# Pinning router setup, conversion starts, two weight splits and the head's load-dependent steps in a scheduled kernel

## Chip, cores and metric

The kernel runs on one core of a Trainium2 chip. The metric is device time in microseconds of one execution; a run gives one such time, and versions are compared by the median of several runs. A core has five engines that each work through an instruction list of their own in order: PE (matmuls; PEld is its weight loads), DVE (vector), ACT (activations), POOL (a second vector engine) and SP, which here issues all DMA transfers. An instruction that waits for another engine or for a transfer holds up everything behind it on its own engine.

## What is computed

Three stages, on 4 x 576 = 2304 tokens of width 512. Attention: for each batch and head, band attention (each query sees the keys less than 4 positions away) plus attention on q, k and v averaged in fours, repeated to full length. Then a softplus MLP with float64 weights, then a top-1 mixture of 8 experts:

```python
x = attn_out.transpose(0, 2, 1, 3).reshape(2304, 512)      # local + downsampled attention
h = x @ w_in; g = np.maximum(h, 0) + np.log1p(np.exp(-np.abs(h))); x = g @ w_out
logits = x @ w_gate + modality_bias[modality_id]; e_idx = argmax(logits)
out[mask] = gate_w[mask] * (np.maximum(x[mask] @ w1[e], 0) @ w2[e])      # for each expert e
```

## The kernel before

**Stages.** Attention is cut into jobs: `Down` (averaged attention of two heads, 16 jobs) and `Local` (band attention of two heads over 192 queries, 48 jobs). Each job has six steps (`st_T`, `st_S`, `st_E`, `st_N`, `st_Ta`, `st_PV`) that are written in the program with fixed lags, so several jobs are in flight. The MLP works on 6 blocks of 384 tokens; a block has 16 chunks of 128 hidden units, each with `mlp_H` (first product and softplus inputs), `mlp_g` (softplus) and `mlp_Y` (second product). Attention of later tokens is woven between the chunks. The expert stage follows.

**The head.** Until `started[0]` is set, only attention of batch 0 and the first of batch 1 is written, with a few conversions near the end. Batch 0 is transposed by PE; from batch 1 on `trans` uses DVE's transpose (line 166), straight from the loaded `qr` and `kr` tiles. A Local job's scores go PE (line 311) -> DVE lines 317 and 319 (mask and maximum) -> ACT line 325 (exponentials) -> DVE 329 and 330 -> POOL 331 (normalise) -> PE 336 (transpose) -> DVE 339 -> PE 344 (product with v, tile `lv`) -> DVE 360.

**Conversion.** The MLP's weights arrive as float64. `from_f64` makes float32 of a 128 x 512 chunk from its integer halves, with one ACT step (line 439) and four DVE steps (lines 440 to 443). 32 chunks, alternating between `wi` and `wo`, must pass before the last chunk of block 0. The raw chunks share six buffers (tag `raw`) with the `qr`, `kr` and `vr` loads of batches 1 to 3, so a load can wait for the conversion, transpose or sum that last read its buffer. `lv` has three buffers, freed by line 344.

**Splits.** From block 1 on every operand is split in a high and a low part (`split`, lines 475 to 480: ACT copies the high part, POOL subtracts for the low part), and a product is three matmuls. Block 0 uses plain float32 matmuls for its first product (line 579) and for half of its second (line 619).

**What sets the order.** The program is written in one order, but the tile framework schedules it: an instruction may move ahead of others on its engine when a timing model in the framework says that its inputs are there. `tc.keep_in_program_order(ins)` forbids this for one instruction: it stays behind the one that was written before it on its engine. Buffers are handed out by the schedule too, so a moved instruction also changes which load waits for what.

Of the kernel before, what the change touches and what calls it, by code (L numbers as in the profile page):

```python
# [9 lines left out]
F32 = mybir.dt.float32  # L10
F32R = mybir.dt.float32r
I32 = mybir.dt.int32
U32 = mybir.dt.uint32
AF = mybir.ActivationFunctionType
ALU = mybir.AluOpType
AX = mybir.AxisListType
# [4 lines left out]
E, FE = 8, 1024  # L21
# [5 lines left out]
NB = NT // TB  # L27
NTT = NT // 128
# [23 lines left out]
NATIVE = 1  # L52
# [3 lines left out]
def band_attention__softplus_mlp__top1_moe(  # L56
# [14 lines left out]
    nc = tc.nc  # L71
    V, A, G, T = nc.vector, nc.scalar, nc.gpsimd, nc.tensor
# [17 lines left out]
    wg = const.tile([128, CC, 32], F32, name="wg")  # L90
    V.memset(wg, 0.0)
    bias_b = const.tile([128, 2, E], F32, name="bias_b")
    bterm = const.tile([128, NTT, E], F32, name="bterm")
# [8 lines left out]
    wi = wpool.tile([128, NC1, CC, 128], F32, name="wi")  # L102
# [3 lines left out]
    def ahead(n):  # L106

        return tc.high_priority(n) if n else nullcontext()
# [12 lines left out]
    class Down:  # L121
# [28 lines left out]
        def pre(self):  # L150
            self.vs = apool.tile([SDH, 2, 2, D], F32, tag="vs", name="vs", bufs=4)
            x = self.raw[2].rearrange("p h a r d -> p (h a) r d")
            o = self.vs.rearrange("p a h d -> p h a d")
            if 4 <= self.b * NPAIR + self.hp < 16:
                G.tensor_tensor(out=x[:, :, 0:2], in0=x[:, :, 0:2], in1=x[:, :, 2:4], op=ALU.add)
                for h in range(2):
                    hs = slice(2 * h, 2 * h + 2)
                    G.tensor_tensor(out=o[:, h], in0=x[:, hs, 0], in1=x[:, hs, 1], op=ALU.add)
            else:
                V.tensor_reduce(out=o, in_=self.raw[2].rearrange("p h a r d -> p h a d r"), axis=AX.X, op=ALU.add)  # L160

        def trans(self, i):

            t = apool.tile([128, S], F32, tag=("qT", "kT")[i], name="qkT", bufs=4)
            if self.b >= PE_TRANSPOSED:
                V.transpose(t, self.raw[i].rearrange("p n d -> p (n d)"))
                return t
            half = RT // 2
            for g in range(2):
                ps = pa("pT")  # L170
                for r in range(half):
                    T.transpose(ps[:, r * RP:(r + 1) * RP], self.raw[i][:, g * half + r].rearrange("p h d -> p (h d)"),
                                ident[:RP, :RP])
                warm(ps)
                o = t.rearrange("m (p r) -> m r p", r=RT)[:, g * half:(g + 1) * half, :]
                x = ps[:, :half * RP].rearrange("m (r p) -> m r p", r=half)
                (A.copy if i or g else V.tensor_copy)(o, x)
            return t
# [81 lines left out]
    def warm(ps):  # L260

        if 4 <= nloc[0] < 12:
            for i in range(1):
                T.matmul(ps[:, 384:384 + 128], ident, ident[:, :128], start=True, stop=True)

    def pa(name):

        if not started[0]:
            nps[0] += 1
            if nps[0] % 2:  # L270
                return psy.tile([128, 512], F32, tag="py", name=name)
        return psa.tile([128, 512], F32, tag="pa", name=name)

    started = [False]
# [158 lines left out]
    def from_f64(raw, dst, on_g):  # L433

        lo, hi = raw[:, :, 0], raw[:, :, 1]
        t = mlp.tile([128, 512], I32, tag="cva", name="cva", bufs=2)
        A.activation(t.bitcast(F32), hi.bitcast(F32), AF.Abs)
        (G if on_g else V).tensor_scalar(t.bitcast(F32), t.bitcast(F32), F64_LEAST, None, ALU.max)  # L440
        V.tensor_scalar(t, t, 3, 0x3FFFFFF8, ALU.logical_shift_left, ALU.bitwise_and)  # L441
        V.scalar_tensor_tensor(t, hi, -0x40000000, t, ALU.bitwise_and, ALU.bitwise_or)  # L442
        V.scalar_tensor_tensor(dst.bitcast(I32), lo, 29, t, ALU.logical_shift_right, ALU.bitwise_or)
# [21 lines left out]
    def conv_to(n):  # L465
        while cpos[0] < min(n, len(conv)):
            i = cpos[0]
            load_raw(i + 2)
            kind, c = conv[i]
            with ahead(0 if started[0] else -50):  # L470
                from_f64(raws.pop(i), wi[:, c].rearrange("p c f -> p (c f)") if kind == "i" else wo[:, c, :], i < 0)
            cpos[0] += 1
            load_raw(i + 2)

    def split(src, tag):
        w = mlp.tile([128, 2] + list(src.shape)[1:], F32R, tag=tag, name=tag, bufs=2)
        with ahead(0):
            A.copy(w[:, 0], src)  # L478
            G.tensor_tensor(out=w[:, 1], in0=src, in1=w[:, 0].bitcast(F32), op=ALU.subtract)  # L479
        return w  # L480

    wis, wos = {}, {}

    def split_wi(n, c):
        if n < NATIVE:
            return
        wis[n, c] = split(wi[:, c] if n < NB else mo["w1"][:, :, c * 128:(c + 1) * 128], "wis")

    def plain_g(n, c):

# [2 lines left out]
    def split_wo(n, c):  # L493
        if plain_g(n, c):
            return
        wos[n, c] = split((wo if n < NB else mo["w2"])[:, c, :], "wos")
# [2 lines left out]


    def router_setup():
        nc.sync.dma_start(out=wg[:, :, :E], in_=w_gate.rearrange("(c p) e -> p c e", p=128))
        nc.sync.dma_start(out=bias_b.rearrange("p m e -> p (m e)"),
                          in_=mod_bias.rearrange("(o m) e -> o (m e)", o=1).to_broadcast([128, 2 * E]))
        ids = mlp.tile([NTT, 128, 2], I32, tag="raw", name="ids", bufs=RAWB)
        idf = mlp.tile([NTT, 128], F32, tag="cvs", name="idf", bufs=2)
        nc.sync.dma_start(out=ids.rearrange("p t w -> p (t w)"), in_=modality.bitcast(I32).rearrange("(p t) -> p t", p=NTT))
        V.tensor_copy(idf, ids[:, :, 0])
        ps = psa.tile([128, 512], F32, tag="pa", name="pI")
        T.transpose(ps[:, :NTT], idf, ident[:NTT, :NTT])  # L510
        is_m = const.tile([128, 2, NTT, 1], F32, name="is_m")
        bt = mlp.tile([128, NTT, E], F32, tag="cvs", name="bt", bufs=2)
        for m in range(2):
            V.tensor_scalar(is_m[:, m, :, 0], ps[:, :NTT], float(m), None, ALU.is_equal)
            G.tensor_tensor(out=bt if m else bterm, in0=is_m[:, m].to_broadcast([128, NTT, E]),
                            in1=bias_b[:, m:m + 1, :].to_broadcast([128, NTT, E]), op=ALU.mult)
        G.tensor_tensor(out=bterm, in0=bterm, in1=bt, op=ALU.add)

    ybuf = {}
# [114 lines left out]
    mo = {}  # L634
# [63 lines left out]
    def quad_weights(q):  # L698

        w1t = mo["w1"]  # L700
        ops = wset[q] = wfree.pop(0)
        tmp = mlp.tile([128, 4, 2, 128], F32, tag="wis", name="wtmp", bufs=2)
        f0, f1 = slice(q * 128, (q + 1) * 128), slice(FE // 2 + q * 128, FE // 2 + (q + 1) * 128)
        a11, a12, a21, a22 = w1t[:, 0:2, f0], w1t[:, 2:4, f0], w1t[:, 0:2, f1], w1t[:, 2:4, f1]

        def split(o, n, src):
            hi = ops[:, 0, o:o + n].rearrange("p o c f -> p (o c) f")
            lo = ops[:, 1, o:o + n].rearrange("p o c f -> p (o c) f")
            A.copy(hi, src)
            G.tensor_tensor(out=lo, in0=src, in1=hi.bitcast(F32), op=ALU.subtract)  # L710

        split(P11, 2, w1t[:, :, f0])
        V.tensor_tensor(out=tmp[:, 0], in0=a21, in1=a22, op=ALU.add)
        V.tensor_tensor(out=tmp[:, 1], in0=tmp[:, 0], in1=a11, op=ALU.subtract)
        split(S1, 2, tmp[:, 0:2].rearrange("p o c f -> p (o c) f"))
        V.tensor_tensor(out=tmp[:, 2], in0=a11, in1=a21, op=ALU.subtract)
        V.tensor_tensor(out=tmp[:, 3], in0=a12, in1=tmp[:, 1], op=ALU.subtract)
        split(S3, 2, tmp[:, 2:4].rearrange("p o c f -> p (o c) f"))
        split(P22, 1, a22)
# [94 lines left out]
    for st in range(12 + LAG):  # L814
        attn_to(pre_end[st])
        if st >= C0 - 5 + LAG:
            conv_to((st - C0 + 5 - LAG) * CR // 4 + 1)
        if st == 9 + LAG:
            split_wi(0, 0)
# [16 lines left out]
    for i, (n, c) in enumerate(seq[:NMLP]):  # L836
# [19 lines left out]
        if i + 1 < NMLP:  # L856
            split_wi(*seq[i + 1])
        else:
            ws = wpool.tile([128, 2, 2, NOP, 2, 128], F32R, tag="wi", name="ws")
            wfree += [ws[:, o] for o in range(2)]  # L860
# [15 lines left out]
        if n == 1 and c == 0:  # L876
            router_setup()
# [93 lines left out]
    p, q, pos_q = stages[-1]  # L971
# [57 lines left out]
```

## Time and profile before

| | |
|---|---|
| median of 3 runs | 795.28 us (795.06 to 795.6) |
| the profiled execution | 798.25 us, of which the span of instructions 796.2 us |
| busy in the span | PE 752.5, DVE 551.7, POOL 472.6, ACT 451.8 us |
| PE idle by stretch | 59:65 us: 5.8; 126:158: 4.4; 212:500: 1.2 |

The span runs from the first to the last instruction; all positions are us from its start. The granted clock of PE is a share of its full speed: 0.50 is 1.2 GHz, 1.00 is 2.4 GHz.

### The profile page before, as it was taken

The page shows a single profiled execution, that of the slowest core. Times are in us where ns is not written, and L with a number is a line of the kernel's source. Part 1 is how long each engine was busy: PE and PEld are TensorE (multiplying, and loading weights), DVE is VectorE, ACT ScalarE, POOL GpSimd, SP SyncE. Part 2 cuts the span into 40 slices and gives each one's busy share as a digit, 9 for nine tenths or more (in the row PEclk, how much of TensorE's full clock was granted, in tenths as well). Part 3 has the DMA queues.
Part 4 walks back from the last instruction along what each step waited for, and adds up shares of the span by engine and source line. Part 5 has one row for each costly group of instructions (what it writes and reads, how often), then busy time and mean ns, then how long its engine had stood idle before and what let it go on. Part 6 is the DMA issues. An engine that isn't in the chain of part 4 may idle for free.

```text
span 796.2 us, 13871 instructions
## 1 busy us (share of the span) xinstructions
PE 752.5 (95%) x4917; PEld 658.4 (83%) x4918; DVE 551.7 (69%) x1103; ACT 451.8 (57%) x1164; POOL 472.6 (59%) x451
## 2 busy tenths in 40 slices
PE   5886998899999999999999999999989999999994
PEld 4664655579799989899999999999977889899893
DVE  6979999967885787988654675556996385275221
ACT  5835566656566646666565656475646265355332
POOL 3435623757776666867566666666689366455541
PEclk9866999999999999999999999999999999999998
DMA  8849666415100251301000100080102022002002
GB/s 195 189 92 274 186 209 178 83 23 116 26 12 16 64 88 31 68 22 51 2 12 12 52 2 1 1 331 1 40 1 79 21 61 80 0 1 80 1 0 84
DMA packets 111448, 55.46 MB, mean 70 GB/s; under 512 B 89594, under 2 KB 102412, under 8 KB 111372
## 3 DMA queue, kind: packets, MB, share of 16 engines
q1 hardware_dynamic: 111371, 54.50, 25.7%
q8 instruction: 41, 0.67, 0.4%
q14 instruction: 36, 0.29, 0.1%
HBM read 45.05 MB, written 9.44 MB: 68 GB/s over the span
## 4 chain that ended last, share of the span: by engine, by line
PE 69%; DVE 17%; issue 4%; ACT 3%; DMA 3%; POOL 2%; SPq 1%; DVEq 0%; POOLq 0%; ACTq 0%
PE py L622 18%; PE ph L582 18%; PE py L913 12%; PE ph L764 9%; PE pO L344 2%; PE pS L311 2%; DVE cva L442 2%; PE ph L579 2%; PE pA L336 2%; DVE cva L440 1%; DVE g L604 1%; PE pS L210 1%; DVE cva L441 1%; DVE g L605 1%; DMA vr<-in_v_dram 1%
## 5 line engine op out<-in xcount | busy, mean ns | idle before, releaser
L622 PE MATMUL py<-g,wos 128*128 128x384 f32 x1056 | 209.8, 341 | 7.2 <-ACT wos L478 4.0
L622 PEld LDWEIGHTS py<-g,wos 128*128 128x128 f32 x1056 | 181.9, 188 | 14.1 <-ACT wos L478 5.2
L582 PE MATMUL ph<-xT,wis 128*128 128x384 f32 x960 | 184.3, 339 | 0.4 <-POOL wis L479 0.4
L582 PEld LDWEIGHTS ph<-xT,wis 128*128 128x128 f32 x960 | 166.3, 188 | 2.7 <-POOL wis L479 1.0
L479 POOL TENSOR_TENSOR wos<-wo,wos 128x512 fp32r<-128x512 f32 x88 | 124.0, 1410 | 40.5 <-ACT wos L478 37.3
L479 POOL TENSOR_TENSOR wis<-wi,wis 128x512 fp32r<-128x512 f32 x80 | 107.1, 1340 | 53.0 <-ACT wis L478 46.4
L588 ACT ACTIVATE ga<-ph 128x384 f32<-128x384 f32 x96 | 46.7, 486 | 72.3 <-PE ph L582 62.6
L603 DVE SCALAR_TENSOR_TENSOR ga<-ph,ga 128x384 f32<-128x384 f32 x88 | 48.4, 550 | 47.5 <-ACT ga L590 47.2
L769 DVE TENSOR_TENSOR u<-ph,u 128x384 f32<-128x384 f32 x60 | 33.2, 555 | 60.3 <-PE ph L764 60.1
L764 PE MATMUL ph<-xs,ws 128*128 128x384 f32 x378 | 73.6, 337 | 1.3 <-DVE u L769 0.9
L325 ACT ACTIVATE ls<-ls,lst 128x70 f32<-128x70 f32 x144 | 49.3, 344 | 43.9 <-DVE lst L319 38.6
L478 ACT CAST wos<-wo 128x512 fp32r<-128x512 f32 x88 | 54.2, 617 | 33.7 <-PE py L622 32.3
L764 PEld LDWEIGHTS ph<-xs,ws 128*128 128x128 f32 x378 | 67.0, 188 | 5.1 <-DVE u L769 1.3
L605 DVE TENSOR_TENSOR g<-ga,g 128x384 fp32r<-128x384 f32 x80 | 69.5, 868 | 1.6
L913 PE MATMUL py<-wos,gs 128*128 128x512 f32 x270 | 68.2, 394 | 0.3 <-ACT gs L773 0.3
L331 POOL TENSOR_TENSOR ls<-ls,lst 128x210 f32<-128x210 f32 x48 | 31.4, 656 | 54.7 <-DVE lst L330 36.8
L604 DVE CAST g<-ga 128x384 fp32r<-128x384 f32 x80 | 58.4, 730 | 4.5 <-PE py L622 0.9
L913 PEld LDWEIGHTS py<-wos,gs 128*128 128x128 f32 x270 | 50.1, 188 | 10.0 <-issue 0.6
L590 ACT ACTIVATE ga<-ga 128x384 f32<-128x384 f32 x96 | 50.3, 524 | 2.0
L589 ACT ACTIVATE ga<-ga 128x384 f32<-128x384 f32 x96 | 50.4, 525 | 0.5
L479 POOL TENSOR_TENSOR wos<-w2s,wos 128x512 fp32r<-128x512 f32 x24 | 33.2, 1388 | 27.5 <-ACT wos L478 27.5
L478 ACT CAST wis<-wi 128x512 fp32r<-128x512 f32 x80 | 48.9, 611 | 0.4 <-PE ph L582 0.4
(163 smaller groups left out, 1293.4 us busy)
## 6 DMA issues: line engine op xcount, KB each, us to landing
raw<-in_moe_w_in_dram SPq DMA_DIRECT2D x16, 512.0 KB
raw<-in_moe_w_out_dram SPq DMA_DIRECT2D x16, 512.0 KB
lv<-in_v_dram SPq DMA_DIRECT2D x72, 70.0 KB
vr<-in_v_dram SPq DMA_DIRECT2D x16, 288.0 KB
ydram<-y SPq DMA_DIRECT2D x12, 384.0 KB
yb<-ydram SPq DMA_DIRECT2D x12, 384.0 KB
out_dram<-ob SPq DMA_DIRECT2D x18, 256.0 KB
qr<-in_q_dram SPq DMA_DIRECT2D x48, 72.0 KB
```

The source lines that it names most:

```text
L325: A.activation(s[:, i, :], s[:, i, :], AF.Exp, bias=st[:, 0, i], accum_out=st[:, 1, i])
L478: A.copy(w[:, 0], src)
L479: G.tensor_tensor(out=w[:, 1], in0=src, in1=w[:, 0].bitcast(F32), op=ALU.subtract)
L582: T.matmul(ps[:, :TB], wt[:, w, cc, :], xT[n][:, x, cc, :], start=(i == 0), stop=(i == 3 * CC - 1))
L589: A.activation(a, a, AF.Exp, scale=-1.0)
L590: A.activation(a, a, AF.Ln, bias=1.0)
L603: V.scalar_tensor_tensor(a, ps[:, :TB], 0.0, a, ALU.max, ALU.add)
L604: (A.copy if n < 1 else V.tensor_copy)(g[:, 0, :], a)
L605: (G if n < 1 else V).tensor_tensor(out=g[:, 1, :], in0=a, in1=g[:, 0, :].bitcast(F32), op=ALU.subtract)
L622: T.matmul(yps[n][dc][:, :TB], w[:, a, dsl], g[:, b, :], start=(c == 0 and i == 0), stop=(c == NC1 - 1 and i == 2))
L764: T.matmul(ps[:, :TB], ops[:, w, a, cc, :], xop[p, x][:, l, cc, :], start=i == 0, stop=i == 5)
L913: T.matmul(yps[n][t], g[:, a, t * 128:(t + 1) * 128], w[:, b, :], start=first and c == q and i == 0, stop=last and c == q + NQ and i == 2)
```

## The change

Pins are put on: the three loads of `router_setup` and its cast and multiplications; the first (ACT) step of every float64 conversion; the two splits of block 1's first two chunks; and, in the head, the first addition of the v sums, the v reductions on DVE and DVE's transposes. No arithmetic is changed.

```diff
@@ pre, trans
-                G.tensor_tensor(out=x[:, :, 0:2], in0=x[:, :, 0:2], in1=x[:, :, 2:4], op=ALU.add)
+                ins = G.tensor_tensor(out=x[:, :, 0:2], in0=x[:, :, 0:2], in1=x[:, :, 2:4], op=ALU.add)
+                if not started[0]:
+                    tc.keep_in_program_order(ins)
...
-                V.tensor_reduce(out=o, in_=self.raw[2].rearrange("p h a r d -> p h a d r"), axis=AX.X, op=ALU.add)
+                tc.keep_in_program_order(
+                    V.tensor_reduce(out=o, in_=self.raw[2].rearrange("p h a r d -> p h a d r"), axis=AX.X, op=ALU.add))
...
-                V.transpose(t, self.raw[i].rearrange("p n d -> p (n d)"))
+                ins = V.transpose(t, self.raw[i].rearrange("p n d -> p (n d)"))
+                if not started[0]:
+                    tc.keep_in_program_order(ins)
@@ from_f64
-        A.activation(t.bitcast(F32), hi.bitcast(F32), AF.Abs)
+        ins = A.activation(t.bitcast(F32), hi.bitcast(F32), AF.Abs)
+        tc.keep_in_program_order(ins)
@@ split, split_wi
-    def split(src, tag):
+    def split(src, tag, pin=False):
...
-        with ahead(0):
-            A.copy(w[:, 0], src)
-            G.tensor_tensor(out=w[:, 1], in0=src, in1=w[:, 0].bitcast(F32), op=ALU.subtract)
+        for ins in (A.copy(w[:, 0], src),
+                    G.tensor_tensor(out=w[:, 1], in0=src, in1=w[:, 0].bitcast(F32), op=ALU.subtract)):
+            if pin:
+                tc.keep_in_program_order(ins)
...
-        wis[n, c] = split(wi[:, c] if n < NB else mo["w1"][:, :, c * 128:(c + 1) * 128], "wis")
+        wis[n, c] = split(wi[:, c] if n < NB else mo["w1"][:, :, c * 128:(c + 1) * 128], "wis",
+                           n == NATIVE and c < 2)
@@ router_setup (pin = tc.keep_in_program_order)
-        V.tensor_copy(idf, ids[:, :, 0])
+        pin(V.tensor_copy(idf, ids[:, :, 0]))
...
-            G.tensor_tensor(out=bt if m else bterm, in0=is_m[:, m].to_broadcast([128, NTT, E]),
-                            in1=bias_b[:, m:m + 1, :].to_broadcast([128, NTT, E]), op=ALU.mult)
+            pin(G.tensor_tensor(out=bt if m else bterm, in0=is_m[:, m].to_broadcast([128, NTT, E]),
+                            in1=bias_b[:, m:m + 1, :].to_broadcast([128, NTT, E]), op=ALU.mult))
```

The number of instructions on each engine stays the same; only their order changes. In the lists below each row is an instruction in the order of its engine, with its line, output and inputs; the numbers are buffer names, equal in both programs. Line numbers of the changed kernel are 3 to 9 higher (317 is 322, 331 is 336, 440 is 446, 291 is 296, 582 is 591, 622 is 631).

**First place: DVE in the head.** Before, from the end of the second conversion; `cva_678` and `wo_96` belong to the third:

```order
L443 SCALAR_TENSOR_TENSOR wi_95<-raw_337,cva_508 128x512
L440 TENSOR_SCALAR cva_678<-cva_678 128x512
L231 RECIPROCAL dsm_467<-dsm_467 96x3
L317 SCALAR_TENSOR_TENSOR ls_585<-pS_577,mask_75 128x210
L441 TENSOR_SCALAR cva_678<-cva_678 128x512
L232 TENSOR_TENSOR de_490<-de_490,dsm_467 96x432
L329 TENSOR_SCALAR lst_555<-lst_555 128x3
L319 TENSOR_REDUCE lst_587<-ls_585 128x3
L442 SCALAR_TENSOR_TENSOR cva_678<-raw_506,cva_678 128x512
L360 TENSOR_TENSOR xN_442<-pO_589,od_392 128x192
L330 RECIPROCAL lst_555<-lst_555 128x3
L443 SCALAR_TENSOR_TENSOR wo_96<-raw_506,cva_678 128x512
```

After, from the same instruction:

```order
L449 SCALAR_TENSOR_TENSOR wi_95<-raw_337,cva_508 128x512
L334 TENSOR_SCALAR lst_587<-lst_587 128x3
L322 SCALAR_TENSOR_TENSOR ls_628<-pS_620,mask_75 128x210
L335 RECIPROCAL lst_587<-lst_587 128x3
L365 TENSOR_TENSOR xN_442<-pO_589,od_392 128x192
L324 TENSOR_REDUCE lst_630<-ls_628 128x3
L334 TENSOR_SCALAR lst_630<-lst_630 128x3
L322 SCALAR_TENSOR_TENSOR ls_672<-pS_664,mask_75 128x210
L335 RECIPROCAL lst_630<-lst_630 128x3
L344 COPY laT_698<-pA_693 70x384
L324 TENSOR_REDUCE lst_674<-ls_672 128x3
L446 TENSOR_SCALAR cva_678<-cva_678 128x512
```

The steps of jobs ls_585, ls_628 and ls_672 now stand ahead of the third conversion. The scores of batch 0 follow each other as ls_553, 585, 628, 672, 722, 767, 808 and 861, in both programs. On POOL, at the same place, before:

```order
L331 TENSOR_TENSOR ls_502<-ls_502,lst_504 128x210
L479 TENSOR_TENSOR wis_1937<-wi_95,wis_1937 128x512
L155 TENSOR_TENSOR vr_662<-vr_662 72x4x128
L479 TENSOR_TENSOR wis_2002<-wi_95,wis_2002 128x512
L158 TENSOR_TENSOR vs_706<-vr_662 72x2x64 x2
L331 TENSOR_TENSOR ls_553<-ls_553,lst_555 128x210
```

And after:

```order
L336 TENSOR_TENSOR ls_502<-ls_502,lst_504 128x210
L336 TENSOR_TENSOR ls_553<-ls_553,lst_555 128x210
L336 TENSOR_TENSOR ls_585<-ls_585,lst_587 128x210
L336 TENSOR_TENSOR ls_628<-ls_628,lst_630 128x210
L155 TENSOR_TENSOR vr_662<-vr_662 72x4x128
L160 TENSOR_TENSOR vs_706<-vr_662 72x2x64 x2
```

The two splits `wis` have left this place; they now stand where block 0 ends.

**Second place: SP's transfers in the head.** Before:

```order
L139 DMA qr_748<-in_q_dram 32x18x32 x4
L139 DMA kr_753<-in_k_dram 32x18x32 x4
L144 DMA vr_758<-in_v_dram 72x4x256
L291 DMA lv_616<-in_v_dram 70x4x64 x3
L139 DMA qr_842<-in_q_dram 32x18x32 x4
L139 DMA kr_847<-in_k_dram 32x18x32 x4
L291 DMA lv_710<-in_v_dram 70x4x64 x3
L144 DMA vr_852<-in_v_dram 72x4x256
```

After:

```order
L139 DMA qr_748<-in_q_dram 32x18x32 x4
L296 DMA lv_616<-in_v_dram 70x4x64 x3
L139 DMA kr_753<-in_k_dram 32x18x32 x3
L296 DMA lv_710<-in_v_dram 70x4x64 x3
L139 DMA kr_753<-in_k_dram 32x18x32
L144 DMA vr_758<-in_v_dram 72x4x256
L139 DMA qr_842<-in_q_dram 32x18x32 x4
L296 DMA lv_838<-in_v_dram 70x4x64 x3
L139 DMA kr_847<-in_k_dram 32x18x32 x4
L144 DMA vr_852<-in_v_dram 72x4x256
```

The `lv` loads, which wait for PE's line 344, stand one to two places further ahead of the `kr` and `vr` loads of batch 1. The buffers differ too: vr_758 now takes the one that the third conversion reads, kr_847 the one of vr_758.

**Third place: PE at the seam between block 0 and block 1.** Line 582 is block 1's first product, line 622 an output product, line 510 a transpose of the router's setup. Before:

```order
L582 MATMUL ph<-xT,wis 128x384 x12
L510 MATMUL pI<-ident,idf 128x18
L311 MATMUL pS<-qkT 64x70 x6
L582 MATMUL ph<-xT,wis 128x384 x12
L622 MATMUL py<-g,wos 128x384 x4
L344 MATMUL pO<-laT,lv 64x64 x6
L622 MATMUL py<-g,wos 128x384 x8
```

After:

```order
L591 MATMUL ph<-xT,wis 128x384 x12
L631 MATMUL py<-g,wos 128x384 x24
L519 MATMUL pI<-ident,idf 128x18
L316 MATMUL pS<-qkT 64x70 x6
L591 MATMUL ph<-xT,wis 128x384 x12
L349 MATMUL pO<-laT,lv 64x64 x6
```

The 24 output products are the last chunk of block 0 and the first of block 1; they now stand ahead of block 1's second chunk.

## Rows read from the trace of the kernel before

**Rows 1.** Busy us of each engine by stretch, PE's granted clock, DMA share, GB/s:

```profile
core 0: us, PE busy (x) PEld busy (x) DVE busy (x) ACT busy (x) POOL busy (x), PEclk, DMA share, GB/s
...
40.00:52.00 12.00, 11.91 (x80) 9.07 (x80) 6.64 (x19) 4.20 (x17) 4.52 (x6) 0.50 0.36 75
...
59.00:65.00 6.00, 0.17 (x3) 0.14 (x2) 4.05 (x10) 2.89 (x12) 2.82 (x5) 0.55 0.97 325
65.00:73.00 8.00, 7.68 (x30) 4.83 (x29) 8.00 (x20) 4.68 (x22) 4.13 (x6) 0.50 0.87 183
...
80.00:126.00 46.00, 46.00 (x241) 27.75 (x239) 45.86 (x101) 27.78 (x80) 20.22 (x17) 1.00 0.63 186
126.00:158.00 32.00, 27.57 (x185) 18.28 (x183) 30.81 (x59) 19.65 (x53) 17.37 (x18) 1.00 0.58 138
...
212.00:500.00 288.00, 286.78 (x2149) 267.28 (x2147) 207.99 (x453) 177.87 (x488) 191.35 (x178) 1.00 0.13 30
```

**Rows 2.** Timeline of DVE in the head (start us, us, instruction):

```profile
26.13 0.38 DVE L317 SCALAR_TENSOR_TENSOR ls<-pS,mask 128x210 f32<-128x210 f32 x1 [0.41 <-PE pS L264]
...
31.02 0.41 DVE L440 TENSOR_SCALAR cva<-cva 128x512 f32<-128x512 f32 x1
...
32.28 0.36 DVE L317 SCALAR_TENSOR_TENSOR ls<-pS,mask 128x210 f32<-128x210 f32 x1
...
35.46 1.50 DVE L440 TENSOR_SCALAR cva<-cva 128x512 f32<-128x512 f32 x1
...
67.79 0.36 DVE L317 SCALAR_TENSOR_TENSOR ls<-pS,mask 128x210 f32<-128x210 f32 x1
...
78.69 0.54 DVE L597 SCALAR_TENSOR_TENSOR gN<-ph,ga 128x384 f32<-128x384 f32 x1
```

**Rows 3.** Timeline of POOL in the head (in brackets: idle before, releaser):

```profile
34.95 1.72 POOL L479 TENSOR_TENSOR wis<-wi,wis 128x512 fp32r<-128x512 f32 x1
...
51.15 1.26 POOL L155 TENSOR_TENSOR vr<-vr 72x512 f32<-72x512 f32 x1
52.49 0.87 POOL L158 TENSOR_TENSOR vs<-vr 72x128 f32<-72x128 f32 x2
53.81 0.67 POOL L185 TENSOR_TENSOR ds<-qkT 128x288 f32<-128x288 f32 x1 [0.45 <-DVE qkT L166]
54.55 0.42 POOL L186 TENSOR_TENSOR dkT<-ds 128x144 f32<-128x144 f32 x1
...
62.10 1.26 POOL L155 TENSOR_TENSOR vr<-vr 72x512 f32<-72x512 f32 x1 [4.30 <-DMA vr<-in_v_dram]
```

**Rows 4.** Timeline of PE in the head:

```profile
40.09 1.15 PE L239 MATMUL pA<-ident,de 96*72 96x96 f32 x6 [2.22 <-DVE lst L329]
...
64.86 1.53 PE L336 MATMUL pA<-ident,ls 128*70 128x128 f32 x6 [5.83 <-POOL ls L331]
...
67.82 1.75 PE L210 MATMUL pS<-dkT,dbd 128*96 128x144 f32 x6
69.36 4.05 PE L579 MATMUL ph<-xN,wi 128*128 128x384 f32 x6
```

**Rows 5.** Timeline of SP: issues of four `kr` transfers in a row:

```profile
41.89 1.94 SPq L139 DMA_DIRECT2D kr<-in_k_dram x4
```

**Rows 6.** Chain of work that ended last: two transfers on it (start us, us):

```profile
137.52 2.17 DMA qr<-in_q_dram
...
151.92 3.39 DMA vr<-in_v_dram
```

**Rows 7.** Timelines of PE, POOL and DVE at the seam of blocks 0 and 1:

```profile
178.93 2.25 PE L582 MATMUL ph<-xT,wis 128*128 128x384 f32 x12
...
181.91 1.02 POOL L605 TENSOR_TENSOR g<-ga,g 128x384 fp32r<-128x384 f32 x1
...
184.69 0.56 DVE L603 SCALAR_TENSOR_TENSOR ga<-ph,ga 128x384 f32<-128x384 f32 x1 [1.52 <-ACT ga L590]
185.28 0.39 DVE L604 CAST g<-ga 128x384 fp32r<-128x384 f32 x1
...
186.64 0.54 DVE L628 COPY y<-py 128x384 f32<-128x384 f32 x1
```

More of the change, by code (lines that the diff above doesn't have):

```diff
@@ L501, in router_setup @@
     def router_setup():
-        nc.sync.dma_start(out=wg[:, :, :E], in_=w_gate.rearrange("(c p) e -> p c e", p=128))
-        nc.sync.dma_start(out=bias_b.rearrange("p m e -> p (m e)"),
-                          in_=mod_bias.rearrange("(o m) e -> o (m e)", o=1).to_broadcast([128, 2 * E]))
+        pin = tc.keep_in_program_order
+        pin(nc.sync.dma_start(out=wg[:, :, :E], in_=w_gate.rearrange("(c p) e -> p c e", p=128)))
+        pin(nc.sync.dma_start(out=bias_b.rearrange("p m e -> p (m e)"),
+                          in_=mod_bias.rearrange("(o m) e -> o (m e)", o=1).to_broadcast([128, 2 * E])))
         ids = mlp.tile([NTT, 128, 2], I32, tag="raw", name="ids", bufs=RAWB)
         idf = mlp.tile([NTT, 128], F32, tag="cvs", name="idf", bufs=2)
-        nc.sync.dma_start(out=ids.rearrange("p t w -> p (t w)"), in_=modality.bitcast(I32).rearrange("(p t) -> p t", p=NTT))
-        V.tensor_copy(idf, ids[:, :, 0])
+        pin(nc.sync.dma_start(out=ids.rearrange("p t w -> p (t w)"), in_=modality.bitcast(I32).rearrange("(p t) -> p t", p=NTT)))
+        pin(V.tensor_copy(idf, ids[:, :, 0]))
         ps = psa.tile([128, 512], F32, tag="pa", name="pI")
```

## Prediction

> **What bounds the kernel now.** I read the page first, where PE, the matmul engine, is by far the busiest, and then the table by stretches of time, for the places where PE waits or runs slowly [rows 1]. In 40:52 and in 65:73 PE's clock is granted at 0.50, and in 59:65 PE does 0.17 us of work. From 80 to 126 us PE is busy 46.00 of 46 us, and DVE 45.86. From 126 to 158 PE idles 4.43 us. In the long middle, 212:500, PE is busy 286.78 of 288. All orders of the two kernels agree again from about 212 us of the old trace (after PE's 818th instruction, DVE's 374th, SP's 170th), so the change acts on the head and on the seam between MLP block 0 and block 1, and what stands after the seam only shifts.
>
> The second view is the timeline of DVE in the head. Scores of attention pass it (line 317) at 26.13 and, two further on, at 32.28: 3.1 us each. Then they slow down, and the last of batch 0 passes at 67.79, seven steps later: 5.1 us each [rows 2]. What stands between is conversion work (lines 440 to 443), issued as soon as it is ready. It also lengthens by itself: line 440 takes 0.41 us at 31.02 and 1.50 at 35.46, while POOL runs the first of two early splits (34.95, 1.72 us) [rows 2, 3]. Here attention waits in line behind work that PE needs much later: conversions of the third and fourth chunk, and weight splits of block 1, which starts at 178.93 [rows 7].
>
> The third view is PE's timeline: it waits 2.22 us before 40.09 and 5.83 us before 64.86, the second for POOL's line 331, which itself stood behind a `vr` addition that waited 4.30 us for its load [rows 3, 4]. The block-0 MLP starts at 69.36 [rows 4].
>
> **The change, part by part.** *Conversions and splits pinned.* Nothing is removed or added; 2 splits (POOL 1.72 us the first) leave the head for the seam, and the conversions follow attention. In the new order the scores of batch 0 stand close together on DVE, POOL and PE. So I give them nearly their old undisturbed step, 2.9 us (3.1 with the filler matmuls of line 264, which the last ones don't have): the last score of batch 0 passes at 32.28 + 7 x 2.9 = 52.6 instead of 67.79. Bounds of the step: 2.5 and 3.4 us, so 49.8 to 56.1.
>
> *What is late next.* Two new waits follow from the new SP order. First, the load of vr_758 now stands behind lv_710. That load needs PE's line 344 on ls_585, which PE issues next to the score of ls_767, five steps after 32.28: 46.8, about 47.8 when it is done. Three lv issues and one kr issue later (four of SP's take 1.94 us [rows 5]) vr_758 is issued at 50; it needs 3.4 us to land (the chain shows 3.39 for such a load [rows 6]; a gap of 4.30 is the high end [rows 3]), so it is there at 53.6. Behind it POOL has 1.26 + 0.87 for the sums, 0.54 for one line 331, then 0.67 + 0.42 for the key sums that PE's first batch-1 score needs [rows 3]: 57.4. PE has run dry at about 51 and restarts slowly, so the score takes 1.5 us, as from 67.82 to 69.36 [rows 4]: the MLP begins at 59.0, which is 10.4 us earlier than 69.36. With the load's high end and the slow step it is 63.9 (gain 5.5); without the lv wait and with 3.39 us it is 56 (gain 13.4).
>
> Slow clock: before, the 8 us after the restart hold attention and most of one chunk at 0.50 [rows 1]; now the same stretch begins with the MLP, so I take back 1.4 us, about what the attention in it (line 344 and one line 336) would have cost at half speed. Bounds 0 and 3. In return 40:52, which was at 0.50, should stay at full clock; that is within the 2.9 us step.
>
> Second, the pinned transposes: DVE's transpose of kr_847 waits for its load, which waits for POOL's sums of vr_758 (55.7 by the sum above), four issues (1.94 us [rows 5]) and 2.2 to 3.4 us of landing [rows 6]: 60 to 61. DVE would be there at about 57.3, so it stands some 3.5 us; everything behind it on DVE stands too: the first batch-1 maximum, fourth conversion, first softplus result gN. I put gN at 67 against 78.69 [rows 2], 11.7 us earlier. That is more than PE's 9.0, so this wait is covered by PE's slow first chunks; if kr_847 comes later than about 63, it shows in full.
>
> *From 80 to 126.* PE is full there, so its earlier start is carried along: 10.4 - 1.4 = 9.0 us. That DVE keeps up I take from its new order: each softplus result now has fewer conversions ahead of it, while conversions are not needed until a chunk or more later.
>
> *From 126 to 158.* PE waits 4.43 us now [rows 1], mostly behind attention steps of DVE that queue behind conversions. With DVE further ahead some of this goes: I take 1.5, between 0 and 4.4.
>
> *The seam.* Now PE follows the first matmuls of block 1 (178.93, 2.25 us) with other ready work: a score and the second chunk of block 1, possible because both splits were made long before. In the new order it does the last chunk's output of block 0 and then the first output of block 1 at once. The low halves of the former need POOL's line 605, done at 182.93 [rows 7]; PE gets there about 181.9: 1.0 us of wait. The latter needs DVE's line 628 twice (0.54 each), then lines 603 (0.56) and 604 (0.39) behind them [rows 7]; from the end of block 0's output this is some 2 us less the 0.7 that overlaps: 1.25. A later matmul waits for its PSUM tile about 0.9, because DVE now takes two transposes whose loads come late ahead of a score. Together 3.2 us, say 3.3; bounds 1.5 and 5.5.
>
> *Router setup.* Two small loads (0.4 to 0.5 us of SP each) move to the seam, where SP is idle, and the additions of the router stay off PE's path; one DVE cast of the ids lies under PE's 2 us of output matmuls. I cost them at nothing; with that cover gone, the cast is at most another 1.5 us, inside the seam's bounds. The pins on the vs sums and the other load-dependent steps bring the POOL and DVE order priced above.
>
> **Sum.** -9.0 - 1.5 + 3.3 = -7.2 us. The profiled execution took 798.25 us for a span of 796.2; it would be 791.05. It stands 2.97 above the median of the runs, 795.28, so the forecast for the median is 788.1.
>
> **Rivals.** *DVE stays the bound: no change.* DVE is as full as PE from 80 to 126 [rows 1]. If the end of the head is set by DVE's total work, only DVE's idle time counts: 5.4 us in 40:52 and 1.95 in 59:65, 7.3 in all, less 3.5 for kr_847 and 1 for the next transposes: 2.8 us won, 3.3 lost at the seam, 795.8. Against it: the last conversions feed chunks that PE reaches 10 to 20 us later. A sentence of the Trainium skill speaks for this rival: Perfetto Trace Analysis, Identifying the Most-Contended Engine, says that matmul busy time is no good measure of how close PE is to its limit, that weight-load busy time is, and that occupancy is a fair measure for Vector. By that rule DVE, not PE, would be the bound in 80:126, since weight loads are busy 27.75 of 46 us there [rows 1]. The trace bears the rule out in part only: the float32 matmuls of that stretch follow each other without a gap, and long matmuls with few weight loads would look the same.
>
> *The pinned transposes stall the head: slower.* kr_847 stands behind lv_838 and vr_758 on SP, with three 512 KB raws next to it. Each us that it lands after 63 costs one us, through DVE, in PE's first outputs. In 59:65 the DMA engines are 0.97 busy [rows 1]; if it lands at 73, as when loads pile up that way, 10 us are gone: 798.1. From 70 on it turns the sign.
>
> *The seam costs little.* If ACT and DVE reach block 1's first g sooner (they have less conversion work behind them) and all of 126:158 is won, the sum is -9.0 - 4.4 + 1.5 = -11.9: 783.4. That the order does not change is excluded: the rows in the section on the change show it.
>
> **Chances.** Forecast (3 to 11 us faster) 0.66, seam cheap or earlier start (over 11) 0.07, DVE bound 0.15 (of it 0.03 faster, 0.10 same, 0.02 slower), transposes 0.12. A difference under 0.2%, 1.6 us, is what the runs of this kernel can't tell from none. So faster 0.76, same 0.10, slower 0.14. The range 782.0 to 795.5 leaves out the slower cases and the far end of the early start; the forecast's own is 784 to 792.3.
>
> **What would show it.** Right: no wait of PE near 38, a granted clock of 1.0 up to about 51; the last batch-0 score near 52; a PE gap of some 6 us ending near 57; MLP start near 59; 80:126 still full; then 2 to 4 us of new PE gaps where block 1 begins. Wrong: a MLP start after 66, DVE standing more than 8 us before a line 169 transpose (it is 166 now), or PE no longer full after 80.

## The result: slower, 1.0073

The changed kernel takes 800.57 us (median of 22 runs, 798.13 to 807.48), the kernel before 795.04 (22 runs, 791.64 to 800.9). The ratio is 1.0073, with an interval of 1.0056 to 1.0090: 5.5 us slower, where 788.1 was forecast, with 782.0 to 795.5 as the range.

First the changed kernel's table by stretches, with the columns of [rows 1]; its profiled execution took 799.57 us.

```profile
40.00:52.00 12.00, 11.58 (x157) 9.18 (x157) 9.96 (x31) 5.66 (x27) 5.01 (x7) 1.00 0.41 77
52.00:59.00 7.00, 0.19 (x5) 0.05 (x1) 7.00 (x18) 3.43 (x15) 3.89 (x6) 0.59 0.66 126
65.00:73.00 8.00, 7.57 (x58) 4.61 (x58) 5.52 (x14) 4.40 (x9) 3.55 (x7) 1.00 0.84 193
80.00:126.00 46.00, 46.00 (x257) 27.60 (x255) 44.69 (x102) 29.03 (x83) 14.55 (x16) 1.00 0.65 201
126.00:158.00 32.00, 25.86 (x164) 17.76 (x162) 31.87 (x65) 21.08 (x57) 13.73 (x11) 1.00 0.51 127
158.00:206.00 48.00, 43.23 (x276) 36.84 (x277) 31.20 (x59) 23.28 (x68) 35.30 (x42) 0.89 0.36 77
212.00:500.00 288.00, 287.56 (x2150) 267.57 (x2151) 204.41 (x456) 177.39 (x489) 193.14 (x179) 1.00 0.13 30
```

The head looks as forecast: 40:52 at full clock, one PE gap, the MLP at work by 65. The loss stands in 126:158, where PE now idles 6.1 us (4.43 before), and in 158:206, where it idles 4.8 and runs part of the time at half clock (0.89 on the mean). PE's timeline has the places:

```profile
59.44 1.76 PE L215 MATMUL pS<-dkT,dbd 128*96 128x144 f32 x6 [7.25 <-POOL dkT L191]
60.99 4.00 PE L588 MATMUL ph<-xN,wi 128*128 128x384 f32 x8
...
154.29 0.52 PE L341 MATMUL pA<-ident,ls 128*70 128x128 f32 x3
154.57 0.94 PE L631 MATMUL py<-g,wos 128*128 128x384 f32 x4
159.35 2.93 PE L631 MATMUL py<-g,wos 128*128 128x384 f32 x8 [3.85 <-POOL g L614]
...
174.72 2.25 PE L591 MATMUL ph<-xT,wis 128*128 128x384 f32 x12
176.81 0.90 PE L631 MATMUL py<-g,wos 128*128 128x384 f32 x4
178.53 1.67 PE L631 MATMUL py<-g,wos 128*128 128x384 f32 x8 [0.82 <-POOL g L614]
182.13 0.98 PE L631 MATMUL py<-g,wos 128*128 128x384 f32 x4 [1.94 <-DVE g L613]
183.69 2.93 PE L631 MATMUL py<-g,wos 128*128 128x384 f32 x8 [0.58 <-DVE g L614]
...
187.66 3.35 PE L591 MATMUL ph<-xT,wis 128*128 128x384 f32 x12
...
192.05 2.36 PE L591 MATMUL ph<-xT,wis 128*128 128x384 f32 x12
...
213.94 0.55 PE L539 MATMUL pL<-ident,lt 128*128 128x128 f32 x3 [0.19 <-DVE lt L536]
```

Line 591 at 174.72 is block 1's first product, line 539 at 213.94 a transpose in the router, behind the seam. In the kernel before they stood at 178.93 [rows 7] and 211.46 in its trace.

Before these are compared: the kernel before was profiled a second time (E12 below), since its first profiled execution took 798.25 us against a median of 795. The second took 792.77. Its rows of the same stretches, and the same four places on PE:

```profile
40.00:52.00 12.00, 10.22 (x128) 8.16 (x128) 11.93 (x28) 4.76 (x22) 7.27 (x12) 0.97 0.67 123
59.00:65.00 6.00, 5.34 (x27) 3.98 (x28) 6.00 (x16) 3.09 (x12) 2.28 (x5) 0.51 0.96 192
80.00:126.00 46.00, 44.39 (x237) 26.61 (x235) 45.83 (x101) 28.57 (x79) 17.37 (x15) 1.00 0.59 187
126.00:158.00 32.00, 29.16 (x175) 20.44 (x173) 27.25 (x50) 19.26 (x55) 21.48 (x21) 0.95 0.43 97
```

```profile
63.85 2.60 PE L579 MATMUL ph<-xN,wi 128*128 128x384 f32 x6
...
158.57 0.52 PE L336 MATMUL pA<-ident,ls 128*70 128x128 f32 x3
...
173.50 2.25 PE L582 MATMUL ph<-xT,wis 128*128 128x384 f32 x12
...
205.99 0.33 PE L530 MATMUL pL<-ident,lt 128*128 128x128 f32 x1 [0.34 <-DVE lt L527]
```

So the first execution's MLP began 5.5 us later (69.36 [rows 4] against 63.85), and its span is 5.5 us longer (796.2 against 790.7). All of its excess over the second lies in the head, where 40:52 ran at 0.50, which is 1.2 GHz, in the first [rows 1] and at 0.97 in the second.

Against the second profile the changed kernel's way is: MLP 2.9 us earlier (60.99 against 63.85); 4.3 earlier at the transpose before the first large wait (154.29 against 158.57); 1.2 later at block 1's first product (174.72 against 173.50), so 5.5 are lost around 155, of which 3.85 are the wait before 159.35 and some 1.3 the eight matmuls behind it (2.93 us, where eight such take 1.67 at 178.53); 8.0 later behind the seam (213.94 against 205.99), another 6.7. Some 1 us comes back later; the spans end 7.0 apart. The medians are 5.5 apart, since the second profile lies 2.3 us below the median of its kernel and the changed kernel's 1.0 below.

### The profile page after: what moved, and what is told of

Same layout as the page of the kernel before. It is cut to its first block, busy times and chain, and to the rows that moved or that the text cites. A ratio compares the mean times of both kernels' runs of the same rounds, so it can differ in the third digit from the quotient of the medians.

```text
span 797.7 us, 13868 instructions
## 1 busy us (share of the span) xinstructions
PE 750.8 (94%) x4917; PEld 657.0 (82%) x4918; DVE 540.7 (68%) x1103; ACT 451.4 (57%) x1164; POOL 465.1 (58%) x451
## 4 chain that ended last, share of the span: by engine, by line
PE 69%; DVE 16%; DMA 4%; POOL 3%; ACT 3%; issue 3%; SPq 1%; DVEq 0%; POOLq 0%; ACTq 0%
PE py L631 19%; PE ph L591 18%; PE py L922 12%; PE ph L773 9%; PE pS L316 2%; PE pO L349 2%; DVE cva L448 2%; PE pA L341 2%; DMA vr<-in_v_dram 2%; DVE cva L446 1%; DVE g L614 1%; PE pS L215 1%; PE pO L253 1%; DMA qr<-in_q_dram 1%; DVE g L613 1%
## 5 line engine op out<-in xcount | busy, mean ns | idle before, releaser
L631 PE MATMUL py<-g,wos 128*128 128x384 f32 x1056 | 212.5, 345 | 11.6 <-POOL g L614 4.9
L631 PEld LDWEIGHTS py<-g,wos 128*128 128x128 f32 x1056 | 183.8, 190 | 19.2 <-POOL g L614 5.8
L484 POOL TENSOR_TENSOR wis<-wi,wis 128x512 fp32r<-128x512 f32 x80 | 106.1, 1327 | 56.4 <-ACT wis L483 52.6
L614 DVE TENSOR_TENSOR g<-ga,g 128x384 fp32r<-128x384 f32 x80 | 71.8, 897 | 1.6
L336 POOL TENSOR_TENSOR ls<-ls,lst 128x210 f32<-128x210 f32 x48 | 28.6, 596 | 45.4 <-DVE lst L335 27.0
L613 DVE CAST g<-ga 128x384 fp32r<-128x384 f32 x80 | 51.4, 642 | 4.6 <-PE py L631 1.1
L588 PE MATMUL ph<-xN,wi 128*128 128x384 f32 x128 | 45.9, 503 | 3.5 <-DVE ls L322 3.1
```

Source lines behind the costliest of these rows:

```text
L613: (A.copy if n < 1 else V.tensor_copy)(g[:, 0, :], a)
L614: (G if n < 1 else V).tensor_tensor(out=g[:, 1, :], in0=a, in1=g[:, 0, :].bitcast(F32), op=ALU.subtract)
L631: T.matmul(yps[n][dc][:, :TB], w[:, a, dsl], g[:, b, :], start=(c == 0 and i == 0), stop=(c == NC1 - 1 and i == 2))
```

## Experiments

All times are medians; each ratio is to the kernel before on the same chip, which took 794.6 us beside E1 to E4, 793.67 beside E5 to E8 and 795.0 beside E9 to E11. Line numbers of the kernels are within a few of the changed kernel's. The last three columns are read from PE's timeline of one profiled execution. That execution can lie off the median (E7's by 5.6 us above, E5's by 2.5 above, E8's by 2.0 above, E9's to E11's by 2.5 to 3.4 below), so what a kernel is worth is read from the ratio, and the columns show only where.

| kernel | us | ratio to before (interval) | MLP begins | block 1's first product | behind the seam |
|---|---|---|---|---|---|
| before, two profiles | 795.04 | | 69.36; 63.85 | 178.93; 173.50 | 211.46; 205.99 |
| changed | 800.57 | 1.0073 (1.0056 to 1.0090) | 60.99 | 174.72 | 213.94 |
| E1 no router pins | 795.3 | 1.0004 (0.9977 to 1.0030) | 60.60 | 174.88 | 207.67 |
| E2 no split pin | 801.7 | 1.0081 (1.0055 to 1.0107) | 60.83 | 174.06 | 214.20 |
| E3 no conversion pin | 795.65 | 0.9997 (0.9972 to 1.0022) | 57.31 | 170.24 | 208.16 |
| E4 no transpose pin | 800.62 | 1.0066 (1.0040 to 1.0092) | 59.47 | 175.53 | 213.51 |
| E5 splits and head only | 789.87 | 0.9952 (0.9930 to 0.9975) | 57.59 | 171.61 | 206.14 |
| E6 splits alone | 794.55 | 0.9995 (0.9973 to 1.0017) | 62.84 | 173.53 | 207.98 |
| E7 router alone | 800.07 | 1.0077 (1.0047 to 1.0107) | 68.68 | 178.91 | 219.06 |
| E8 conversions alone | 795.29 | 1.0017 (0.9996 to 1.0038) | 62.97 | 176.77 | 210.68 |
| E9 pI from the other pool | 795.62 | 1.0001 (0.9977 to 1.0026) | 60.55 | 175.00 | 206.62 |
| E10 changed, less clamp | 795.53 | 0.9995 (0.9968 to 1.0023) | 61.12 | 168.31 | 205.01 |
| E11 before, less clamp | 796.8 | 1.0013 (0.9984 to 1.0042) | 62.31 | 174.38 | 206.89 |

### The seam: which pin costs there, and how

**E1.** The router's pins are taken back, all others stay:

```diff
-        pin(V.tensor_copy(idf, ids[:, :, 0]))
+        V.tensor_copy(idf, ids[:, :, 0])
```

and so for its three loads and its multiplications.

> The changed kernel without the pins of the router's setup (three loads, one cast, two multiplications); all other pins stay. Its PE order where block 1 begins is again nearly that of the kernel before: the first output of block 1 comes after its second chunk. Theory A (the router's pins, not the splits, set the new PE order there; its waits of 0.82, 1.94 and 0.58 us and the half clock behind them cost some 6 us): 4 to 7 us faster than the changed kernel, 0.998 to 1.002 of the kernel before. Theory B (the splits' return to this place costs it): within 2 us of the changed kernel, 1.005 to 1.010 of the kernel before.

Measured: 1.0004. Up to block 1's first product the run is the changed kernel's (174.88 against 174.72), and from there to behind the seam it takes 32.8 us instead of 39.2 (213.94 - 174.72); the second profile of before takes 32.5. Theory A. In the lists of instructions one pin does it: with the cast alone pinned, PE, DVE, ACT and POOL stand as in the changed kernel, and with all but the cast pinned they stand as in E1. Neither variant was run.

**E2.** The splits' pin is taken back (`split` is that of the kernel before again).

> The changed kernel without the pin of block 1's first two splits: they return to POOL and ACT in the head, and the PE order where block 1 begins stays that of the changed kernel. Theory A (router's pins): within 2 us of the changed kernel, 1.005 to 1.010 of the kernel before, and PE still waits for DVE's lines 612 to 614 there. Theory B (splits): POOL's two splits no longer run beside DVE's softplus steps, the waits of 3.3 us and the half clock go, 4 to 7 us faster than the changed kernel.

Measured: 1.0081, no gain; the seam takes 40.1 us. PE's longest wait there is 2.43 us, for DVE's line that is 613 in the changed kernel. Theory B falls.

**E7.** The kernel before with the router's pins alone.

> The kernel before with the router's pins and nothing else; the splits of block 1 are still made in the head. PE's order where block 1 begins is that of the changed kernel. Theory A (the router's pins make that order, and its waits and half clock cost by themselves): 4 to 7 us slower than the kernel before, 1.005 to 1.009, with PE waiting 2 to 4 us between 180 and 195. Theory B (the order costs only when the splits stand there too): within 2 us of the kernel before.

Measured: 1.0077, as large a loss as that of the change, with the splits still in the head. The seam takes 40.2 us (219.06 - 178.91). The profiled execution took 805.66 us, 5.6 above the median of its runs; it begins the MLP late, at 68.68, as the first profile of before does. PE's clock is 1.00 in 158:206 of this run, so the half clock is no part of it here; the waits do it, of which two of PE's are these:

```profile
182.96 1.67 PE L623 MATMUL py<-g,wos 128*128 128x384 f32 x8 [1.06 <-POOL g L606]
187.06 2.38 PE L623 MATMUL py<-g,wos 128*128 128x384 f32 x12 [2.44 <-DVE g L605]
```

**E9.** Why should a cast of 0.21 us on DVE move PE's order? Its transpose writes the PSUM tile `pI`, which takes its turn among four buffers with the tiles of scores and of first products. All pins stay, and only this tile comes from elsewhere:

```diff
-        ps = psa.tile([128, 512], F32, tag="pa", name="pI")
+        ps = psy.tile([128, 512], F32, tag="py", name="pI")
```

> The changed kernel with all its pins, the router's cast of the ids among them; only the PSUM tile pI of the router's transpose comes from the other pool, so that the tiles of the next score and of block 1's second chunk no longer follow it in the rotation of four buffers. Theory I (the pinned cast costs through that rotation): PE's order where block 1 begins is again score, second chunk, then outputs; 4 to 7 us faster than the changed kernel, 0.998 to 1.002 of the kernel before. Rival J (the cast costs through its place on DVE): within 2 us of the changed kernel.

Measured: 1.0001. PE's timeline of E9 at the seam:

```profile
175.00 2.24 PE L591 MATMUL ph<-xT,wis 128*128 128x384 f32 x12
177.17 0.58 PE L316 MATMUL pS<-qkT 64*64 64x70 f32 x12
177.69 0.97 PE L631 MATMUL py<-g,wos 128*128 128x384 f32 x4
178.55 0.62 PE L591 MATMUL ph<-xT,wis 128*128 128x384 f32 x2
...
192.50 3.49 PE L631 MATMUL py<-g,wos 128*128 128x384 f32 x16 [0.30 <-DVE g L614]
...
206.62 0.49 PE L539 MATMUL pL<-ident,lt 128*128 128x128 f32 x3
```

The score (line 316) follows the first product at once, and the only wait left is 0.30 us. The cast itself begins at the same time on DVE; here it is in the changed kernel, and then in E9:

```profile
183.56 0.21 DVE L517 CAST idf<-ids 18x128 f32<-18x128 int32 x1
```

```profile
183.55 1.30 DVE L517 CAST idf<-ids 18x128 f32<-18x128 int32 x1
```

So Theory I holds, and rival J falls. The pinned cast stays behind everything that is written before it on DVE, so `pI` is held late, and the next score and the second chunk, which follow it in the rotation, are held with it. PE is left with output products whose inputs DVE and POOL are still making.

### Around 155 us: conversions and what waits for them

In the changed kernel, DVE's last step of a conversion (line 449), SP's issue of the value load behind it, and POOL's sum and what follows:

```profile
148.66 0.68 DVE L449 SCALAR_TENSOR_TENSOR wo<-raw,cva 128x512 int32<-128x512 int32 x1
```

```profile
149.41 0.31 SPq L144 DMA_DIRECT2D vr<-in_v_dram  x1
```

```profile
153.32 3.78 POOL L155 TENSOR_TENSOR vr<-vr 72x512 f32<-72x512 f32 x1 [5.47 <-DMA qr<-in_q_dram]
157.07 1.28 POOL L484 TENSOR_TENSOR wos<-wo,wos 128x512 fp32r<-128x512 f32 x1
158.31 0.99 POOL L614 TENSOR_TENSOR g<-ga,g 128x384 fp32r<-128x384 f32 x1
```

The 29th conversion ends at 149.34 and frees a raw buffer; SP issues the load at 149.41; POOL, idle for 5.47 us (the row names a later transfer of the same queue as the releaser; its buffer comes from the next conversion), sums it from 153.32 to 157.10, and only then makes the low half for which PE waits until 159.35. In the second profile of before the 29th conversion ends at 137.02, and the same sum runs at 140.72. The conversions are 12 us later while PE is 4 us earlier.

**E3.** The pin on the conversions' first step is taken back.

> The changed kernel without the pin on the first step of each conversion: conversions float ahead of attention again in the head. Theory C (what PE gains in the head is given back near 155 us, because the last conversions end when DVE is done with them, at 156 us in both kernels): the MLP starts some 5 to 10 us later than at 61, but PE's wait near 155 us shrinks with it, so the time stays within 3 us of the changed kernel. The reading of the prediction (the head's gain is carried to the end): 6 to 10 us slower than the changed kernel, 1.015 or more of the kernel before.

Measured: 0.9997, some 5 us faster than the changed kernel. Both expectations miss: the MLP begins not later but 3.7 us sooner, at 57.31. The wait near 155 is gone (the 29th conversion ends at 140.17, the sum of that load runs at 143.59), but PE waits elsewhere instead (2.30 us at 69.04 for the first softplus result, and four times 0.57 to 1.17 us from 134 to 150), so that from the MLP's start to block 1 it takes 112.9 us against 113.7. What E3 gains lies in the head (3.7 us) and at the seam (37.9 us against 39.2), hardly between them. What the pin costs in the head is seen on PE and SP of E3:

```profile
55.76 1.75 PE L215 MATMUL pS<-dkT,dbd 128*96 128x144 f32 x6 [4.39 <-POOL dkT L191]
```

```profile
44.92 0.32 SPq L144 DMA_DIRECT2D vr<-in_v_dram  x1
```

The value load vr_758 goes out at 44.92, in the changed kernel at 51.01. There it stands behind lv_710 on SP, as the order in the section on the change shows, and takes the buffer of the third conversion, which ends at 48.50; here it stands ahead of lv_710, and the third conversion ends at 39.20. So attention is fed sooner when conversions may go ahead of it.

**E4.** The pins on the head's transposes are taken back.

> The changed kernel without the pins on DVE's transposes of the head. Rival D (DVE standing in front of a pinned transpose whose load is late is what costs): DVE's idle time between 52 and 73 us goes down by 3 us or more, the conversions end 3 us sooner, and the time falls by 3 us or more against the changed kernel. Theory C with the seam as the larger loss: the transposes wait somewhere in any order, within 2 us of the changed kernel.

Measured: 1.0066, 800.62 us: nothing. DVE's idle time between 52 and 73 us goes from 4.4 us to 3.5 only, and the last conversion ends at 156.6, no sooner than the changed kernel's (155.98). Rival D falls.

**E8.** The kernel before with the conversions' pin alone.

> The kernel before with the first step of every conversion pinned and nothing else; in the head attention goes first on DVE, the splits stay on POOL there. The prediction's reading (attention first is a gain that is kept): the MLP begins by 62, 4 us or more faster than the kernel before, 0.995 or less. Theory C (the later conversions are missed near 155 us, by about what the head won): the MLP begins by 62, the last conversion ends at 155 or later, POOL waits 4 us or more for a value load near 150, and the time is within 3 us of the kernel before.

Measured: 1.0017. The last conversion ends at 156.74, POOL idles 5.10 us and sums the late value load at 153.72, PE waits 3.78 us for POOL's `g` before 160.12, and 0.9 us of lead at the MLP's start have become 3.3 of delay at block 1 (176.77 against 173.50; this execution is 2.0 us above its median, the second profile of before 2.3 below). Theory C, except that the MLP begins at 62.97 instead of by 62.

**E10 and E11.** To take DVE's work away, the clamp of tiny weights runs on 16 of 512 columns, in the changed kernel and in the kernel before:

```diff
-        (G if on_g else V).tensor_scalar(t.bitcast(F32), t.bitcast(F32), F64_LEAST, None, ALU.max)
+        V.tensor_scalar(t.bitcast(F32)[:, :16], t.bitcast(F32)[:, :16], F64_LEAST, None, ALU.max)
```

> The changed kernel, with the clamp of tiny weights in each conversion (line 446) on 16 of its 512 columns only, so that the clamp is left out for the others; 32 steps of 0.41 us on DVE become short, some 10 us of DVE work. Theory C (the rate at which DVE delivers conversions decides when the value loads get their buffers, and so PE's wait near 155 us): conversions end by 151, that wait of 3.85 us falls below 1.5, 3 to 7 us faster than the changed kernel. Rival K (ACT's pinned order decides, not DVE's work): conversions end within 2 us of 156, the time within 2 us of the changed kernel.

> The kernel before with the same edit (the clamp of tiny weights on 16 of 512 columns). If PE's work bounds the kernel before from 80 us on, as the prediction took it, only its waits from 126 to 158 (4.4 us) can shrink: 0 to 3 us faster than the kernel before. If DVE's conversions bound it there too (rival L), 4 to 9 us faster, 0.989 to 0.995.

Measured: the step takes 0.17 us instead of 0.41, which makes 32 x 0.24, some 8 us, and not the 10 expected. The changed kernel gains some 5 us (0.9995 where it was 1.0073), the kernel before nothing (1.0013). In E10 the 29th conversion ends at 144.29, 5 us sooner, POOL's sum starts at 147.76, and the wait of 3.85 us is gone, with one of 1.59 us for DVE at 155.92 in its place; block 1 begins 6.4 us sooner (168.31), in an execution that is 3.4 us below its median. The last conversion ends at 155.54, so that part of the expectation misses: what counts is the conversion whose buffer the load takes, not the last. E11 shows the other side, in its row of the table by stretches:

```profile
126.00:158.00 32.00, 29.16 (x171) 20.03 (x170) 20.90 (x41) 16.93 (x48) 18.85 (x21) 0.89 0.32 60
```

DVE is busy 20.90 us where it was 27.25 in the second profile of before, and PE's 29.16 is the same. In 80:126 DVE is still busy for 45.59 of 46 us: it runs further ahead, and nothing comes of it. So before, DVE's work does not bound; the change made it bind.

### Do the two costs add, and what gains

**E5.** The split pin and the head's pins are kept, the router's and the conversions' are taken back.

> The kernel with the split pins and the pins of the head's sums and transposes, without those of the router's setup and of the conversions. The two removals gave 5.3 and 5.0 us against the changed kernel when each was made alone. Theory E (two separate costs, one where block 1 begins and one near 155 us): they add, about 790 us, 0.992 to 0.996 of the kernel before. Rival F (one loss in two places: what is won near 155 is lost again where block 1 begins): 794 to 796 us, 0.998 to 1.002 of the kernel before.

Measured: 789.87 us, 0.9952 (0.9930 to 0.9975). By the ratios of E1 and E3 the two removals would come to 0.9928, so they add, or nearly, and this version beats both kernels, by 3.8 and by some 10 us.

**E6.** The kernel before with the splits' pin alone.

> The kernel before with the two splits of block 1 pinned and nothing else; conversions still stand ahead of attention on DVE. Theory G (POOL's two splits in the head, and the DVE steps that run slowly beside them, are what delays attention): PE's wait near 38 us goes, the MLP begins at 62 us or sooner, 3 to 7 us faster than the kernel before, 0.991 to 0.996. Rival H (attention stands behind the conversions, as the prediction has it): the MLP begins within 3 us of 69, the time within 2 us of the kernel before.

Measured: 0.9995. Theory G falls: the MLP begins at 62.84, 1.0 us sooner than in the second profile of before, and nothing is left of it. At the seam PE now waits for the split itself, ACT's line 477:

```profile
177.90 0.62 PE L584 MATMUL ph<-xT,wis 128*128 128x384 f32 x2 [0.56 <-ACT wis L477]
```

The seam takes 34.5 us, as in E5, against 32.5 in the kernel before; in E1, which pins the splits too, it takes 32.8, and why it differs was not tried. Rival H holds for the time, though its bound on the MLP's start was set by the first profile. So the gain of E5 needs the head's pins; whether it needs the split pin beside them, and which of the head's pins makes it, was not tried.

### The kernel before once more

**E12.**

> The kernel before, unchanged, for a second profile: the first profiled execution took 798.25 us, about 3 us more than the median of its runs. If that is a spread in the head (the stretches at half clock up to 73 us), this profile's MLP begins 1 to 4 us sooner and the rest follows with the same distances; if it is spread over the whole span, no stretch differs by more than 1 us.

Measured: 792.77 us. The MLP begins 5.5 us sooner, more than the 1 to 4 expected, and the distances behind it are the same (109.6 and 109.7 us to block 1, 32.5 and 32.5 over the seam). It is one execution; the median lies between the two.

## Why the prediction was wrong

**The new order of the head was read rightly.** The last batch-0 score passes DVE at 52.59 (52.6 forecast), vr_758 is issued at 51.01 (50), the MLP begins at 60.99 (59.0), kr_847 is transposed at 61.48 (60 to 61), the first softplus result comes at 67.07 (67):

```profile
52.59 0.36 DVE L322 SCALAR_TENSOR_TENSOR ls<-pS,mask 128x210 f32<-128x210 f32 x1
...
61.48 0.78 DVE L169 STREAM_TRANSPOSE qkT<-kr 128x576 f32<-128x576 f32 x1 [1.92 <-DMA kr<-in_k_dram]
...
67.07 0.55 DVE L606 SCALAR_TENSOR_TENSOR gN<-ph,ga 128x384 f32<-128x384 f32 x1
```

**First failed step: what it was compared with.** "10.4 - 1.4 = 9.0 us" and "In return 40:52, which was at 0.50, should stay at full clock" took the half clock of one execution as the kernel's own. The second profile has no such stretch there, and the MLP at 63.85: against it the head gains 2.9 us, against the first 8.4 (69.36 - 60.99) of the 10.4 that were forecast for the MLP's start. An execution at the median lies between the two. The text had the warning in hand, 2.97 us above the median, and took it off at the end as a constant; it lay in the very stretch where the gain was claimed.

**Second failed step: "conversions are not needed until a chunk or more later".** Their results are not; their buffers are. The pinned start brings the conversions up to 12 us later, the value loads wait for the buffers, POOL waits for the loads, and PE for POOL: instead of 1.5 us won in 126:158, 5.5 were lost up to block 1 (E8, E10). "That DVE keeps up" failed here, not in PE's first chunks. The late load is not the whole of it: in E3 and E5 it is gone, and from the MLP's start to block 1 PE still takes 112.9 and 114.0 us, against 109.6 in the kernel before, since it waits for DVE and POOL elsewhere. So in none of these orders does PE carry its earlier start whole to block 1.

**Third: the seam, 3.3 forecast, 6.7 measured, and for another reason.** The waits of the new outputs come to 0.82 + 1.94 + 0.58 = 3.34 us, the sum that was priced, but partly by luck: 0.82 for POOL where 1.0 was put, 2.52 for DVE's `g` where 1.25 was, and no wait for a PSUM tile where 0.9 was. What was not priced follows them: the half clock (granted 0.57 in 182:190; 2.93 us for eight matmuls that take 1.67, 3.35 for twelve that take 2.36, 2.3 us in these two rows) and, where it doesn't occur (E7), later waits for DVE and ACT of 1.66 and 1.70. And the order was put down to the splits, "possible because both splits were made long before". E2 and E7 show the same order and loss with the splits made early; it was the router's cast, which stood in the sum at nothing (E1, E9). What the late splits add where the cast is free, up to 2 us in E5 and E6, is small beside it.

**The rivals.** "DVE stays the bound" is wrong for the kernel before (E11) and in part right for the changed one (E10). The rule on the most-contended engine in the Trainium skill (Perfetto Trace Analysis, Identifying the Most-Contended Engine) would put DVE ahead of PE in 80:126 by weight-load busy time; E11, where some 8 us of DVE's work are taken away and nothing is gained, speaks against it here. The pinned transposes, the slower rival, cost nothing that E4 can tell. The sum by the measured terms, against the second profile: -2.9 (head) - 1.4 (from there to 154 us) + 5.5 (around 155) + 6.7 (seam) - 1 (behind it) = 6.9, for a span that is 7.0 longer.

## What to carry to other kernels

A profiled execution that lies above its median has its excess somewhere: take a second profile before pricing a gain in a stretch at half clock. A pin on a small instruction also holds its buffers, in SBUF (a load waits for the late conversion) and in PSUM (a score waits for a late transpose): follow the rotation of each tile that it reads or writes, not the instruction's 0.2 us. And undo a bundle of pins one by one; of these, two cost about 5 us each and hid a gain of 0.5%.

## What the runs showed of the hardware

The same wait of PE can be followed by either clock. Here is the same instruction on PE's timeline in the second profile of before, and then in E7:

```profile
38.67 0.66 PE L239 MATMUL pA<-ident,de 96*72 96x96 f32 x6 [1.41 <-DVE lst L329]
```

```profile
38.41 0.66 PE L239 MATMUL pA<-ident,de 96*72 96x96 f32 x6 [1.41 <-DVE lst L329]
```

After the first, 40:52 is granted 0.97, after the second 0.50 (1.2 GHz). What decides was not found.

POOL's sum of 72x512 took 3.78 us at 153.32 in the changed kernel, beside four of DVE's conversion steps (lines 448 and 449) that took 0.64 each. In E3 at 143.59 it took 1.27 us, and the DVE step beside it (line 448, at 143.67) took 1.75 where the same step takes 0.68 at 147.14. The Trainium skill (SBUF — State Buffer, Who interferes with whom) says that a DVE instruction with two inputs in SBUF and a GpSimd instruction that reads SBUF lock each other out, the one that starts first holding the port. That one of the two is lengthened agrees with it; which one held the port is not shown, since POOL's row begins 0.10 us before DVE's in the changed kernel, where POOL's is the long one, and 0.08 us before in E3, where DVE's is. No run tested it by itself.
